# Top-k attention and a squared-ReLU MoE in one program: thresholds compared as bfloat16 views, late range check in other buffers, flag earlier, new order table

## The chip, the cores and the metric

The program runs on one core of a Trainium2 chip. The metric is the device time of one execution in microseconds (us), median of three. The engines are named as in the profile: PE is TensorE (PEld its weight loads), DVE VectorE, ACT ScalarE, POOL GpSimd, SP SyncE, which here issues the DMAs.

## What is computed

The reference, cut to what matters. `q`, `k`, `v` are (8, 8, 576, 64) in float32; the two MoE weight matrices arrive as float64.

```python
def _attn_ref(q, k, v):
    scores = (1.0 / np.sqrt(D)) * np.matmul(q, k.transpose(0, 1, 3, 2))
    kth = np.partition(scores, -32, axis=-1)[..., -32:-31]
    scores = np.where(scores >= kth, scores, -1000000000.0)
    attn = np.exp(scores - np.max(scores, axis=-1, keepdims=True))
    attn = attn / (np.sum(attn, axis=-1, keepdims=True) + 1e-09)
    return np.matmul(attn, v)

def _moe_ref(x, w_in, w_out, s, b):        # x: 4608 x 512, d_ff 2048
    r = np.maximum(x @ w_in, 0.0)
    return (s * (r * r) + b) @ w_out
```

So each of 8 x 8 x 576 score rows keeps its 32 largest entries, takes a softmax over them, and multiplies V; the result, laid out as 4608 tokens of 512, goes through two dense layers.

## The kernel before

**The work.** Attention is cut into 288 tiles of 128 score rows. For a tile, PE makes 128 x 576 scores in two halves (L418, `s_ps`), ACT copies them to SBUF with the scale (L424, tile `sc`), and DVE finds the 32nd largest in steps: the eight largest of each of eight groups of 72 (L429, `cand`), two picks over those (L434), a negated reduction (L438, `nt`), the row maximum (L453, `nb`) and the eight largest of 31 negated values (L444, `wl`), whose last entry is minus the threshold guess. `half_at` (L458, POOL) turns the high 16 bits of that entry, read as an int16, into a bias. `side` (L464, ACT) takes the sign of bias minus each score's high 16 bits, and counts; `window` (L470, POOL) multiplies scores and signs, `pad` (L474, POOL) adds eight padding values that depend on the count, and `wmax` (L484, DVE) reads the exact 32nd value from the eight largest of the product. `expo` (L478, ACT) makes the exponentials and `mask` (L488, DVE) keeps the chosen ones and sums them. PE transposes (L515 `tp`, L520 `tq`), ACT and DVE split the result into a high and a low part (L525, L530, L535, L540), and PE multiplies V (L550 to L556, `av`). At the end of a pair of heads, `finish1` to `finish5` scale by the sums and write a piece of the MoE input to DRAM (`xd`).

The MoE runs in 18 blocks of 256 tokens, each of 16 chunks of 128 hidden units. One chunk is 12 matmuls into `h` (L665), a ReLU (L671) and a square (L674) on ACT, a high and a low part on POOL (L678 `gh`, L682 `gl`), and 6 matmuls into `ops` (L688). After a block's last chunk DVE makes `osb` (L696) and SP stores it (L703). A block can start when the pairs that hold its tokens have been written.

The two weight matrices come as 64-bit words in 64 loads of 256 KB; DVE turns each into float32 in three bit operations (`bits0` to `bits2`, L342 to L348), ACT and POOL split it (L351, L354). All of that stands in the first part of the program, beside the first 40 tiles or so. When the second matrix is complete, PE sums its columns (L391, 32 matmuls).

**The range check.** The conversion is only valid for numbers in a range. So, late in the program, all 64 pieces are loaded once more (`again`, L326 in `fetch`) into buffers of the ring `sc`, which also holds the attention scores, the MoE input of block 16 (the list `LATE`) and the very last `osb`; ACT squares them (`far0`, L364) and squares and sums them (`far1`, L373; one instruction for a piece of the first matrix, two for the second). DVE takes the maximum (L1119), and `flag0` (DVE, L1123 to L1126), `flag1` (PE, L1130) and `flag2` (DVE, L1133 and L1134) join it with a check of the thresholds into one number `flag`. Behind the program every engine loads the flag (L1295) and branches on it (L1296): a general path would run if it were set. With these inputs it isn't.

**The order.** All instructions are recorded in a graph and a list scheduler, `Graph.order`, places them, engine by engine, before anything is emitted. `PARTS` gives for each operation its engine, a slot, a duration and an offset in tiles that is added to the tile's number to make a due key; `SLACK` says by engine how much later an operation with an earlier key may start and still go first; `TURN0` and `TURNS` set the key of a MoE chunk in tiles, `WTURN` that of the weights, `CHECK` that of the range check. Buffers are rings (`BUFS`: 5 `sc`, 2 `qs`, 2 `ka`, one `h`, two `ops`). Up to the first MoE matmul the program also fills gaps that the plan shows on PE with matmuls that nobody reads (`keep_busy`, L383).

```python
        lim = min(x[0] for x in c) + slack[e]
        return min(((o.key, s, o) for s, o in c if s <= lim), key=lambda x: x[:2])[1:]
```

On the engines themselves everything runs strictly in the emitted order, with semaphore waits between engines.

## Time and profile before

| | |
|---|---|
| time, median of 3 (lowest to highest) | 1493.95 us (1493.13 to 1495.11) |
| profiled execution: its own time | 1495.7 us |
| its span from first to last instruction | 1493.9 us, mean granted clock 0.986 |
| PE busy | 1433.2 us, 96% of the span |
| DVE, ACT, POOL busy | 1261.7 (84%), 1283.4 (86%), 1150.9 us (77%) |
| DMA | 256.6 MB, mean 172 GB/s |

The profiled execution is one run with the hardware profiler; its own time is 0.12% above the median of the others, and its span leaves 1.8 us of it outside. Busy times are sums over the whole span: a share says nothing about a stage. How the stages differ is read from a view by stretches, and what holds an engine in one from the timeline and from the chain of waits. A PE that counts as busy may still run its matmuls further apart than it could.

### The profile page before, as it was taken

What the parts mean: (1) busy time and instruction counts of PE and PEld (TensorE: products, weight loads), DVE (VectorE), ACT (ScalarE), POOL (GpSimd) and SP (SyncE); (2) the same over time, 40 slices, a digit from 0 to 9 for tenths busy, and PEclk for the clock granted to TensorE, in tenths of its full rate; (3) what the DMA queues carried; (4) which work ended last, traced back from release to release, by engine and by line L of the source; (5) the groups of instructions that cost most, each with busy time, mean ns of one, the idle gap of its engine ahead of it and who ended that gap; (6) DMA issues with size and microseconds to landing.
All of it is one profiled execution on the core that took longest, in us unless ns stands there. A gap on an engine that the chain in (4) does not pass through costs nothing.

```text
span 1493.9 us, 34308 instructions
## 1 busy us (share of the span) xinstructions
PE 1433.2 (96%) x9468; PEld 1263.4 (85%) x9468; DVE 1261.7 (84%) x5527; ACT 1283.4 (86%) x3382; POOL 1150.9 (77%) x1920
## 2 busy tenths in 40 slices
PE   6977999999999999999999999999999999999996
PEld 5744678999989899988898989999899989989885
DVE  6988998999999999999999999889999987875000
ACT  6777888998999899989999999888998998888366
POOL 6877887888888878888888788877888877675532
PEclk9987999999999999999999999999999999999998
DMA  6776766666566665676666665666566555552144
GB/s 184 221 204 180 221 179 172 179 177 191 159 178 195 182 171 155 187 211 174 177 195 196 170 182 163 192 175 168 157 197 185 149 176 139 145 167 87 45 151 134
DMA packets 173735, 256.63 MB, mean 172 GB/s; under 512 B 41952, under 2 KB 83936, under 8 KB 173536
## 3 DMA queue, kind: packets, MB, share of 16 engines
q1 hardware_dynamic: 173536, 254.37, 59.6%
q8 instruction: 78, 1.28, 0.4%
q14 instruction: 121, 0.99, 0.2%
HBM read 181.67 MB, written 72.61 MB: 170 GB/s over the span
## 4 chain that ended last, share of the span: by engine, by line
PE 73%; DVE 8%; ACT 8%; POOL 4%; DMA 4%; issue 2%; SPq 0%; POOLq 0%; DVEq 0%; ACTq 0%
PE ops L688 21%; PE h L665 21%; PE s_ps L418 10%; PE tp L515 7%; PE av L554 3%; PE av L555 3%; PE av L550 2%; PE tq L520 2%; DVE cand L429 1%; DVE sc L488 1%; DVE chk L484 1%; DMA kr<-in_kq_dram 1%; ACT sg L464 1%; DMA out_dram<-osb 1%; ACT sc L373 1%
## 5 line engine op out<-in xcount | busy, mean ns | idle before, releaser
L429 DVE MAX8 cand<-sc 128x8 f32<-128x72 f32 x2304 | 410.2, 221 | 37.1 <-ACT sc L424 35.7
L470 POOL TENSOR_TENSOR wt<-sc,sg 128x576 f32<-128x576 f32 x288 | 371.6, 1290 | 75.9 <-ACT sg L464 44.2
L665 PE MATMUL h<-x,wih 128*128 128x256 f32 x2176 | 427.7, 289 | 1.9 <-ACT rt L671 1.3
L665 PEld LDWEIGHTS h<-x,wih 128*128 128x128 f32 x2176 | 350.5, 190 | 21.5 <-ACT rt L671 4.6
L665 PE MATMUL h<-x,wil 128*128 128x256 f32 x1088 | 306.8, 282 | 0.0
L418 PE MATMUL s_ps<-ka,qs 128*128 128x288 f32 x1024 | 244.6, 321 | 27.9 <-ACT sc L424 11.0
L424 ACT ACTIVATE sc<-s_ps 128x288 f32<-128x288 f32 x576 | 233.5, 405 | 29.0 <-PE s_ps L418 23.8
L464 ACT ACTIVATE sg<-sc,nb 128x576 bf16<-128x576 int16 x288 | 222.5, 773 | 25.5 <-POOL nb L458 20.4
L484 DVE MAX8 chk<-wt 128x8 f32<-128x584 f32 x288 | 219.3, 761 | 23.2 <-POOL wt L474 20.8
L488 DVE SCALAR_TENSOR_TENSOR sc<-sc,chk,e 128x576 f32<-128x576 f32 x288 | 232.3, 807 | 7.4 <-ACT e L478 5.1
L478 ACT ACTIVATE e<-sc,nb 128x576 f32<-128x576 f32 x288 | 213.5, 741 | 25.7 <-DVE sc L488 18.2
L682 POOL TENSOR_TENSOR gl<-rt,gh 128x256 fp32r<-128x256 f32 x288 | 212.6, 739 | 27.3 <-PE ops L688 8.8
L418 PEld LDWEIGHTS s_ps<-ka,qs 128*128 128x128 f32 x1024 | 165.5, 193 | 70.9 <-ACT sc L424 39.0
L688 PE MATMUL ops<-woh,gh 128*128 128x512 f32 x576 | 202.3, 411 | 5.7 <-DVE osb L696 5.2
L665 PEld LDWEIGHTS h<-x,wil 128*128 128x128 f32 x1088 | 206.2, 190 | 0.0
L678 POOL TENSOR_SCALAR gh<-rt 128x256 fp32r<-128x256 f32 x288 | 116.7, 406 | 108.0 <-PE ops L688 50.3
L688 PE MATMUL ops<-woh,gl 128*128 128x512 f32 x576 | 196.3, 403 | 0.4 <-POOL gl L682 0.4
L688 PE MATMUL ops<-wol,gh 128*128 128x512 f32 x576 | 195.0, 404 | 0.0
L530 DVE TENSOR_TENSOR pl<-tp,ph 128x512 fp32r<-128x512 f32 x252 | 172.5, 684 | 23.4 <-ACT ph L525 20.4
L515 PE MATMUL tp<-idr,sc 128*128 128x128 f32 x1152 | 176.6, 276 | 3.5 <-DVE sc L488 1.6
L525 ACT ACTIVATE ph<-tp 128x512 fp32r<-128x512 f32 (+1 forms) x288 | 170.4, 592 | 5.3 <-PE tp L515 3.2
L671 ACT ACTIVATE rt<-h 128x256 f32<-128x256 f32 x288 | 109.2, 379 | 50.8 <-PE h L665 46.6
(151 smaller groups left out, 2941.5 us busy)
## 6 DMA issues: line engine op xcount, KB each, us to landing
ka<-kd SPq DMA_DIRECT2D x240, 288.0 KB, 4.4
vd<-vst SPq DMA_DIRECT2D x56, 320.0 KB, 3.9
vst<-vd SPq DMA_DIRECT2D x56, 320.0 KB, 3.2
kr<-in_kq_dram SPq DMA_DIRECT2D x56, 288.0 KB, 3.5
kd<-kh SPq DMA_DIRECT2D x56, 288.0 KB, 3.8
kd<-kr SPq DMA_DIRECT2D x56, 288.0 KB, 3.3
qs<-kd SPq DMA_DIRECT2D x224, 64.0 KB, 2.3
out_dram<-osb SPq DMA_DIRECT2D x36, 256.0 KB, 2.2
```

Source lines behind the costliest of these rows:

```text
L418: nc.tensor.matmul(t.ps[:, :SH], st, kx[:, cs], start=(m == 0), stop=(m == last))
L424: nc.scalar.activation(t.sc[:, hf * SH : (hf + 1) * SH], t.ps[:, :SH], AF.Identity, scale=scale)
L429: nc.vector.max(t.cand[:, g, 1:9], t.sc[:, g * GW : (g + 1) * GW])
L464: nc.scalar.activation(t.sg, t.sc.bitcast(I16)[:, 1::2], AF.Sign, bias=t.half, scale=-1.0, accum_out=t.cnt[:, 0:1])
L470: nc.gpsimd.tensor_tensor(out=t.wt[:, :S], in0=t.sc, in1=t.sg, op=ALU.mult)
L478: nc.scalar.activation(t.e, t.sc, AF.Exp, bias=t.nb)
L484: nc.vector.max(t.pair.chk[:, t.i, 0:PADS], t.wt)
L488: nc.vector.scalar_tensor_tensor(t.sc, t.sc, chk[:, PADS - 1 : PADS], t.e, op0=ALU.is_ge, op1=ALU.mult, accum_out=chk[:, PADS : PADS + 1])
L515: nc.tensor.transpose(tp[:, c, :], t.sc[:, c * P : (c + 1) * P], idf)
L665: nc.tensor.matmul(k.h, wi_at(a, cc, fc * P, P), k.x[cc][:, c, :], start=(cc == 0 and i == 0), stop=(cc == NCC - 1 and i == 2))
L682: nc.gpsimd.tensor_tensor(out=k.gl[fc], in0=k.rt[fc], in1=k.gh[fc].bitcast(F32), op=ALU.subtract)
L688: nc.tensor.matmul(k.ops[t], g[fc][:, t * P : (t + 1) * P], wo_at(w, fc, 0, DM), start=(fc == 0 and i == 0), stop=(fc == NFC - 1 and i == 2),)
```

## The change

It does five things.

1. `half_at` moves from POOL to DVE: a `tensor_reduce` over one element, the high half of the entry read as a bfloat16, negated.
2. `side` reads the high halves of the scores as bfloat16 instead of int16, and its scale is -1 - 2^-9 instead of -1. The threshold check in `finish1` and `flag0` becomes a minimum against 1e-30 instead of a maximum against 32767.
3. The range check loads its pieces into the rings `qs` and `ka` (those of Q and K) in turn, two buffers each, instead of `sc`.
4. The keys of the flag go down (`flag0` from 60 to -20.96, in tiles), and `flag2` is given a duration of 9000 ns in the plan.
5. All slots, durations and offsets of `PARTS`, the slacks and the three turns are new, so that nearly every instruction has another place.

```diff
-    "half": ("POOL", 147, 190, 44.13), "side": ("ACT", 759, 860, -18.51), "win": ("POOL", 1250, 1290, -12.54),
+    "half": ("DVE", 62, 150, 40.88), "side": ("ACT", 759, 860, -45.29), "win": ("POOL", 1250, 1290, -42.12),
...
-    "glow": ("POOL", 705, 745, 56.08), "o": ("PE", 231, 395, 42.40), "wagain": ("SP", 920, 3900, 44.77), "flag0": ("DVE", 560, 640, 60.00), "flag1": ("PE", 110, 360, 50.77), "flag2": ("DVE", 420, 500, 23.67), "osb": ("DVE", 654, 738, -13.89), "store": ("SP", 450, 2300, -30.67),
+    "glow": ("POOL", 705, 745, 60.00), "o": ("PE", 231, 395, 41.19), "wagain": ("SP", 920, 3900, 45.57), "flag0": ("DVE", 560, 640, -20.96), "flag1": ("PE", 110, 360, 31.04), "flag2": ("DVE", 420, 9000, 18.37), "osb": ("DVE", 665, 750, -9.98), "store": ("SP", 450, 2300, 1.71),
...
-SLACK = {"PE": 26, "DVE": 33, "ACT": 43, "POOL": 120, "SP": 861}
-TURN0, TURNS = 33.0, 1.074
-WTURN = 50.4
+SLACK = {"PE": 0, "DVE": 53, "ACT": 92, "POOL": 111, "SP": 520}
+TURN0, TURNS = 34.5, 1.136
+WTURN = 48.1
...
+    def again_in(n):
+        return ("qs", "ka")[n % 2]
...
         def again(w):
-            w.fetch(sb.tile([P, 2 * WCH], I32, name="sc", tag="sc", bufs=BUFS["sc"]))
+            tag = again_in(w.n)
+            w.fetch(sb.tile([P, 2 * WCH], I32, name=tag, tag=tag, bufs=BUFS[tag]))
...
-        nc.gpsimd.tensor_scalar(t.half, t.wl.bitcast(I16)[:, 15:16], 1.0, 32767.5, op0=ALU.mult, op1=ALU.add)
+        nc.vector.tensor_reduce(t.half, t.wl.bitcast(BF16)[:, 15:16], axis=AX.X, op=ALU.max, negate=True)
...
-            t.sg, t.sc.bitcast(I16)[:, 1::2], AF.Sign, bias=t.half, scale=-1.0, accum_out=t.cnt[:, 0:1]
+            t.sg, t.sc.bitcast(BF16)[:, 1::2], AF.Sign, bias=t.half, scale=-1.0 - 2.0**-9, accum_out=t.cnt[:, 0:1]
...
-        key, raw = CHECK + n / 2, Buf("sc")
+        key, raw = CHECK + n / 2, Buf(again_in(n))
...
-        nc.vector.scalar_tensor_tensor(tm, tx, 32767.0, tm, op0=ALU.is_lt, op1=ALU.mult)
+        nc.vector.scalar_tensor_tensor(tm, tx, 1.0e-30, tm, op0=ALU.is_gt, op1=ALU.mult)
```

How that moves instructions shows at three places. Lines of the changed kernel are three higher than those of before from L364 on (L458 is L461 there).

The end of DVE's order; `osb` is the last block's result, `far` the sums of the range check, `tmin` the thresholds. Before:

```order
L696 SCALAR_TENSOR_TENSOR osb<-ops,cols,bias 128x512 x4
L1119 TENSOR_REDUCE cols<-far 128x1
L696 SCALAR_TENSOR_TENSOR osb<-ops,cols,bias 128x512 x2
L1123 TENSOR_REDUCE cols<-tmin 128x1
L1124 TENSOR_REDUCE cols<-tmin 128x1
L1125 SCALAR_TENSOR_TENSOR cols<-cols 128x1
L1126 SCALAR_TENSOR_TENSOR cols<-cols 128x1
L1133 TENSOR_REDUCE cols<-tp 1x1
L1134 TENSOR_SCALAR flag<-cols 1x1
L1295 TENSOR_LOAD flag
```

and in the change:

```order
L699 SCALAR_TENSOR_TENSOR osb<-ops,cols,bias 128x512 x2
L1122 TENSOR_REDUCE cols<-far 128x1
L1126 TENSOR_REDUCE cols<-tmin 128x1
L1127 TENSOR_REDUCE cols<-tmin 128x1
L1128 SCALAR_TENSOR_TENSOR cols<-cols 128x1
L1129 SCALAR_TENSOR_TENSOR cols<-cols 128x1
L1136 TENSOR_REDUCE cols<-tp 1x1
L1137 TENSOR_SCALAR flag<-cols 1x1
L699 SCALAR_TENSOR_TENSOR osb<-ops,cols,bias 128x512 x2
L1298 TENSOR_LOAD flag
```

The flag is finished ahead of the last block's two `osb`. On PE its transpose, the last matmul of all before, now has 66 `h` and 48 `ops` matmuls behind it.

ACT's order near its end; `rt<-h` is a ReLU, `rt<-rt` a square, the rest is range check. Before, up to the load of the flag:

```order
L671 ACTIVATE rt<-h 128x256
L373 ACTIVATE sc,far<-sc,cols 128x128 x2
L674 ACTIVATE rt<-rt 128x256
L364 ACTIVATE sc<-sc 128x256 x2
L373 ACTIVATE sc,far<-sc,cols 128x128 x4
L1295 TENSOR_LOAD flag
```

and in the change, around the last two pieces:

```order
L674 ACTIVATE rt<-h 128x256
L367 ACTIVATE qs<-qs 128x256
L677 ACTIVATE rt<-rt 128x256
L376 ACTIVATE qs,far<-qs,cols 128x128 x2
L367 ACTIVATE ka<-ka 128x256
L376 ACTIVATE ka,far<-ka,cols 128x128 x2
L674 ACTIVATE rt<-h 128x256
L677 ACTIVATE rt<-rt 128x256
```

The last piece was checked behind the last of the 288 chunks; now seven chunks follow it. Of the 64 pieces, 37 stood behind chunk 273 before, all in the last block; now the first two stand behind chunk 247 and the 64 are spread over 34 chunks, about two to a chunk.

PE's order where the column sum (`av<-woh,ones`) begins, which needs the whole second weight matrix. Before:

```order
L665 MATMUL h<-x,wih 128x256 x2
L665 MATMUL h<-x,wil 128x256
L418 MATMUL s_ps<-ka,qs 128x288 x2
L391 MATMUL av<-woh,ones 128x512
L391 MATMUL av<-wol,ones 128x512
```

and in the change:

```order
L668 MATMUL h<-x,wih 128x256 x2
L668 MATMUL h<-x,wil 128x256
L691 MATMUL ops<-woh,gh 128x512 x2
L421 MATMUL s_ps<-ka,qs 128x288 x2
L394 MATMUL av<-woh,ones 128x512
L394 MATMUL av<-wol,ones 128x512
```

Ahead of it PE has issued the transposes of 37 tiles and the `h` matmuls of 13 chunks before, of 36 tiles and 15 chunks in the change. The second MoE block begins after 42 tiles before, and after 39 in the change; the ninth after 169 and 166; the seventeenth after 288 and 287. The matmuls that only fill gaps are 203 before and 172 in the change. On DVE the last of the 64 weight conversions stands behind 37 masks before and 36 in the change.

## Rows read from the trace of the kernel before

**Rows 1.** The page, busy time and share of each engine over the span.

```profile
PE 1433.2 (96%) x9468; PEld 1263.4 (85%) x9468; DVE 1261.7 (84%) x5527; ACT 1283.4 (86%) x3382; POOL 1150.9 (77%) x1920
```

**Rows 2.** Busy time of each engine by stretches of the span, named in the header.

```profile
core 0: us, PE busy (x) PEld busy (x) DVE busy (x) ACT busy (x) POOL busy (x), PEclk, DMA share, GB/s
0.00:187.00 187.00, 148.18 (x759) 103.67 (x759) 161.93 (x731) 140.73 (x352) 143.25 (x235) 0.91 0.69 202
187.00:1195.00 1008.00, 1001.42 (x6848) 904.53 (x6847) 951.32 (x4205) 915.34 (x2346) 835.11 (x1387) 1.00 0.63 178
1195.00:1382.00 187.00, 184.45 (x1246) 167.10 (x1245) 142.40 (x580) 163.22 (x457) 128.23 (x224) 1.00 0.50 143
1382.00:1434.00 52.00, 51.70 (x333) 46.84 (x333) 1.98 (x4) 17.27 (x46) 26.00 (x45) 1.00 0.15 49
1434.00:1482.00 48.00, 47.20 (x288) 41.19 (x286) 1.56 (x3) 46.80 (x183) 18.34 (x32) 1.00 0.62 190
1482.00:1493.90 11.90, 0.27 (x1) 0.08 (x1) 2.50 (x9) 0.00 (x0) 0.00 (x0) 0.66 0.14 51
```

**Rows 3.** Timeline, 1481 us to the end: start, duration, engine, line, instruction.

```profile
1481.28 0.62 PE L688 MATMUL ops<-woh,gl 128*128 128x512 f32 x2
1481.71 0.20 ACT L373 ACTIVATION_READ_ACCUMULATOR sc<-sc,cols 128x1 f32 x1
1481.94 0.25 DVE L1119 TENSOR_REDUCE cols<-far 128x1 f32<-128x96 f32 x1 [39.95 <-ACT sc L373]
1482.11 1.40 DVE L696 SCALAR_TENSOR_TENSOR osb<-ops,cols,bias 128x512 f32<-128x512 f32 x2
1482.88 1.00 SPq L703 DMA_DIRECT2D out_dram<-osb  x2
1484.83 0.14 DVE L1134 TENSOR_SCALAR flag<-cols 1x1 int32<-1x1 f32 x1
```

**Rows 4.** Instructions of lines 1295, 1296 and 1330: durations in ns, start in us.

```profile
L1295 PEldq TENSOR_LOAD <-flag x1: 482/482/482, 1485.0 to 1485.0; - x1
L1296 SPq COMPARE_BRANCH  x1: 50/50/50, 1485.5 to 1485.5; - x1
L1296 PEldq COMPARE_BRANCH  x1: 3772/3772/3772, 1485.6 to 1485.6; - x1
L1330 SPq DRAIN  x3: 7/7/13, 1490.3 to 1493.2; - x3
L1330 PEldq DRAIN  x2: 8/8/8, 1492.6 to 1493.2; - x2
```

**Rows 5.** SP's timeline near the end: loads of block 16 (L642) and the range check (L326).

```profile
1370.03 7.94 SPq L642 DMA_DIRECT2D sc<-xd  x4
...
1396.15 0.38 SPq L326 DMA_DIRECT2D sc<-in_moe_w_in_dram  x1
1430.00 1.76 SPq L326 DMA_DIRECT2D sc<-in_moe_w_out_dram  x4
```

**Rows 6.** The chain that ended last, near 1421 us: start, duration, work.

```profile
1421.12 1.43 PE h L665 x12
1422.56 1.39 PE ops L688 x6
1423.94 1.43 PE h L665 x12
```

**Rows 7.** DVE's timeline near 14 us.

```profile
14.32 0.14 DVE L453 TENSOR_REDUCE nb<-nt 128x1 f32<-128x8 f32 x1
14.38 0.18 DVE L444 MAX8 wl<-nt 128x8 f32<-128x31 f32 x1
14.48 0.62 DVE L429 MAX8 cand<-sc 128x8 f32<-128x72 f32 x4
```

**Rows 8.** Groups of instructions by line: busy us, mean ns of one, idle before.

```profile
L464 ACT ACTIVATE sg<-sc,nb 128x576 bf16<-128x576 int16 x288 | 222.5, 773 | 25.5 <-POOL nb L458 20.4 <-POOL wt L470 2.9
L478 ACT ACTIVATE e<-sc,nb 128x576 f32<-128x576 f32 x288 | 213.5, 741 | 25.7 <-DVE sc L488 18.2 <-DVE avu L617 2.6 <-DVE avu L624 2.5
L458 POOL TENSOR_SCALAR nb<-wl 128x1 f32<-128x1 int16 x288 | 54.9, 191 | 39.3 <-DVE wl L444 17.1 <-PE tq L520 1.1
L453 DVE TENSOR_REDUCE nb<-nt 128x1 f32<-128x8 f32 x288 | 42.8, 149 | 2.0
L674 ACT ACTIVATE rt<-rt 128x256 f32<-128x256 f32 x288 | 120.1, 417 | 2.7
L671 ACT ACTIVATE rt<-h 128x256 f32<-128x256 f32 x288 | 109.2, 379 | 50.8 <-PE h L665 46.6 <-POOL gl L682 1.5 <-POOL qs L837 0.6
```

**Rows 9.** Timelines of DVE, POOL and PE where the last weights are made, and the second block's start.

```profile
216.36 0.40 DVE L348 SCALAR_TENSOR_TENSOR pl<-pl,s_ps 128x256 int32<-128x256 int32 x1
...
217.92 0.73 POOL L354 TENSOR_TENSOR wol<-pl,woh 128x256 fp32r<-128x256 f32 x1
...
221.42 0.40 PE L391 MATMUL av<-woh,ones 128*128 128x512 f32 x1
...
247.31 0.46 PE L665 MATMUL h<-x,wih 128*128 128x256 f32 x2
```

More of the change, by code (lines that the diff above doesn't have):

```diff
@@ L14 @@
 I32 = mybir.dt.int32
-I16 = mybir.dt.int16
 AF = mybir.ActivationFunctionType
@@ L55 @@
-    "exp": ("ACT", 667, 748, 55.25), "wmax": ("DVE", 668, 754, -35.90), "pad": ("POOL", 480, 420, -5.48), "mask": ("DVE", 731, 815, -58.93),
-    "put": ("PE", 436, 680, 1.41), "putq": ("PE", 108, 350, 13.37), "high": ("ACT", 478, 595, 55.65), "low": ("DVE", 590, 675, -3.19),
-    "resth": ("ACT", 264, 372, 17.15), "restl": ("DVE", 568, 610, -43.14), "av": ("PE", 146, 320, -18.63), "avout": ("ACT", 320, 470, -18.43),
-    "eps": ("ACT", 95, 200, -14.34), "recip": ("DVE", 72, 180, 23.03),
-    "sums": ("DVE", 140, 230, 34.96), "add": ("POOL", 1375, 1420, -57.27), "spread": ("POOL", 525, 560, -55.31), "turn": ("PE", 108, 352, -31.85),
@@ L66 @@
-SLACK = {"PE": 26, "DVE": 33, "ACT": 43, "POOL": 120, "SP": 861}
-TURN0, TURNS = 33.0, 1.074
-WTURN = 50.4
+    "wload": ("SP", 1000, 4400, 15.06), "bits0": ("DVE", 325, 415, 40.39), "bits1": ("DVE", 321, 412, 38.69), "bits2": ("DVE", 321, 404, 16.54),
+    "colsum": ("PE", 7400, 7600, -9.49), "far0": ("ACT", 322, 430, 17.89), "far1": ("ACT", 507, 524, 29.35), "far2": ("ACT", 782, 793, 5.64),
+    "whigh": ("ACT", 322, 425, -32.98), "wlow": ("POOL", 700, 736, -59.18), "farmax": ("DVE", 170, 250, 32.68), "bias": ("ACT", 695, 700, -17.80),
@@ new lines @@
+    "vload": ("SP", 620, 3600, -28.72), "vhigh": ("ACT", 360, 466, 11.55), "vlow": ("POOL", 840, 875, 50.14), "vkeep": ("SP", 600, 2800, 57.18),
+    "qk": ("PE", 132, 300, -35.38), "sc": ("ACT", 291, 408, -35.29), "group": ("DVE", 134, 218, 57.78),
+    "m1": ("DVE", 92, 180, -45.24), "m2": ("DVE", 93, 180, 37.54), "neg": ("DVE", 120, 203, 19.40), "low8": ("DVE", 100, 182, 16.84), "max": ("DVE", 60, 143, -26.78),
+    "half": ("DVE", 62, 150, 40.88), "side": ("ACT", 759, 860, -45.29), "win": ("POOL", 1250, 1290, -42.12),
@@ new lines @@
+    "exp": ("ACT", 667, 748, 48.70), "wmax": ("DVE", 668, 754, -40.73), "pad": ("POOL", 480, 420, -16.83), "mask": ("DVE", 724, 807, -8.69),
+    "put": ("PE", 436, 680, -1.29), "putq": ("PE", 108, 350, 9.09), "high": ("ACT", 478, 595, 40.24), "low": ("DVE", 590, 675, -40.93),
+    "resth": ("ACT", 264, 372, 11.07), "restl": ("DVE", 568, 610, -43.39), "av": ("PE", 146, 320, -33.81), "avout": ("ACT", 320, 470, -4.23),
+    "eps": ("ACT", 192, 298, -21.24), "recip": ("DVE", 78, 168, 13.84),
+    "sums": ("DVE", 125, 207, 13.95), "add": ("POOL", 1375, 1420, -58.41), "spread": ("POOL", 525, 560, -51.94), "turn": ("PE", 108, 352, -31.37),
@@ new lines @@
+    "scale": ("DVE", 325, 405, -15.53), "xkeep": ("SP", 500, 2600, 31.13),
+    "xload": ("SP", 460, 2700, -33.79), "xhigh": ("ACT", 306, 405, -31.38), "xlow": ("POOL", 692, 732, -60.00),
+    "h": ("PE", 357, 523, 38.72), "relu": ("ACT", 263, 378, -55.75), "square": ("ACT", 306, 415, -34.00), "ghigh": ("POOL", 369, 405, 60.00),
+    "glow": ("POOL", 705, 745, 60.00), "o": ("PE", 231, 395, 41.19), "wagain": ("SP", 920, 3900, 45.57), "flag0": ("DVE", 560, 640, -20.96), "flag1": ("PE", 110, 360, 31.04), "flag2": ("DVE", 420, 9000, 18.37), "osb": ("DVE", 665, 750, -9.98), "store": ("SP", 450, 2300, 1.71),
+}
@@ L572, in finish1 @@
         nc.vector.tensor_reduce(tmin[:, 0, pr.i : pr.i + 1], pr.chk[:, :n, PADS - 1 :], axis=AX.XY, op=ALU.min)
-        nc.vector.tensor_reduce(tmin[:, 1, pr.i : pr.i + 1], pr.nb[:, 1, :n], axis=AX.X, op=ALU.max)
+        nc.vector.tensor_reduce(tmin[:, 1, pr.i : pr.i + 1], pr.nb[:, 1, :n], axis=AX.X, op=ALU.min)
     def finish1a(pr):
```

19 lines of the change are left out of this document (5 added, 14 removed).

## The prediction

> **What bounds the kernel now.** I read the busy shares first: PE is at 96%, the others between 77% and 86% [rows 1]. A share of the whole span hides stages, so the next view is the one by stretches [rows 2]. It shows four regimes. Up to 187 us PE is busy for 148 of 187 us, at a mean granted clock of 0.91, and DVE for 162: this is the start, where DVE converts weights beside the first tiles. From 187 to 1195 us PE idles 6.6 us in 1008 and DVE 56.7: PE sets the time and DVE follows at 94%. From 1382 us attention is over (DVE 2 us of 52), and PE runs MoE chunks alone. From 1434 to 1482 us ACT is busy 46.8 of 48 us, where it was busy 17 of 52 in the stretch ahead. Behind 1482 us nearly nothing runs for 11.9 us.
>
> The chain of waits gives the price of a chunk: 1.43 us of `h` and 1.39 us of `ops`, 2.82 us from one chunk to the next [rows 6]. So 16 chunks need 45.1 us, and 288 need 812 us.
>
> The reader should see in the timeline of the end that PE's last MoE matmul ends at about 1481.9 us, that ACT's last range check ends at the same time, and that the flag is finished at 1484.97 us, 3.1 us later, behind a maximum, two `osb` of 1.40 us together and six short steps on DVE and PE [rows 3]. Only then do the engines load it and branch. PE is the slowest in that: its load takes 0.48 us and its branch 3.77 us, and its first drain stands at 1492.6 us, against 1490.3 us for SP [rows 4]. From the flag to the end of the span it is 8.9 us.
>
> **The change part by part.** The sum is made against the profiled execution, whose time is 1495.7 us, its span 1493.9 us and the 1.8 us around it; the median of the runs shown is 1493.95 us, 1.75 us lower, and I subtract the sum from that. A measurement of this kernel tells about 0.2%, 3.0 us, from no change.
>
> *The flag ahead of the end.* In the new order the flag is done ahead of the last two `osb`, and 66 `h` and 48 `ops` matmuls follow its transpose on PE: 66 x 1.43/12 + 48 x 1.39/6 = 19 us. So PE can load the flag as soon as its last matmul is issued, at about 1481.9 us in the times of before, not at 1485.0: 3.1 us less, and the 8.9 us behind it stay. What is late next is SP: it issues the last stores until 1483.9 us [rows 3], and from its branch at 1485.5 us to its drain it took 4.8 us [rows 4], so its drain would come at 1488.7 us, ahead of PE's at 1489.5. PE stays last. Gain 3.0 us, nothing at the least (a flag that comes late holds PE instead), and no more than 3.1. The Trainium skill (Runtime: NRT & Kernel Launch, Instruction fetch mechanics) says that a taken branch to a page that isn't at hand has to fetch it by DMA first; by that rule the branch stays dear however early the flag is, and PE's 3772 ns, against 482 for its load, agree [rows 4].
>
> *The range check in other buffers.* Before, block 16 held four of the five `sc` buffers: its loads went out at 1370 us, one piece was loaded at 1396 us, and the next four at 1430 us [rows 5]. So 37 pieces fell into the last block, where ACT is full [rows 2]. From 1434 to 1482 us PE had 48 us for 45.1 us of chunks plus what it was behind with; I put the loss to ACT at 2.6 us at most. In the new order two pieces fall to a chunk: 46.8 us less 16 x (0.38 + 0.42) us of ReLU and square [rows 8] leaves 34 us for 37 pieces, 0.92 us each, so ACT has 1.9 x 0.92 + 0.8 = 2.5 us in 2.82, 90% in place of 98%. It is spread over two blocks, so some loss stays. Gain 1.5 us, between 0 and 2.6. The cover is ACT's idle time of 35 us between 1382 and 1434 us [rows 2]; without it, nothing is gained. SP issues the pieces between the loads of blocks 16 and 17, and a piece that waits for its buffer holds those loads behind it; block 17's come some 16 chunks ahead of their use.
>
> *The threshold on DVE.* POOL loses 288 instructions of 191 ns [rows 8], at 77% busy: nothing. DVE gains 288 small reductions. The nearest row is the one-element reduction of `nb`: it lasts 149 ns [rows 8], and the next instruction starts 60 ns behind it [rows 7]. I take 60 ns, since DVE is in order and rarely waits for its own result there, and keep 149: 17 to 43 us over the program. Of that 37 tiles fall into the start, 2.2 to 5.5 us. The other 251, 15 to 37 us, fall into stretches in which DVE idles 56.7 + 44.6 us [rows 2]; I cost them at nothing, with that idle time as cover. If the cover fails, see the rivals. In the new order the reduction often stands behind a mask, so that the sign waits 0.8 us more; ACT's wait for the old one was 20.4 us in all [rows 8], off PE's path. The sign itself stays at 773 ns; the exponential, as long and on float32, takes 741 [rows 8], so its 288 could at best give back 9 us of ACT, which isn't the bound.
>
> *The new order of the start.* The column sum waits for the last weights. Before, DVE made the last of them at 216.8 us, POOL at 218.7, and PE began the sum at 221.4 [rows 9]. In the new order DVE has as much ahead of that point, less one tile and plus the 2.2 to 5.5 us. PE has two chunks more ahead of it, 5.6 us, and one tile less. A tile costs PE about (1433.2 - 812)/288 = 2.1 us, an upper estimate that takes all that isn't MoE as tiles [rows 1, 6]. So at an equal point PE is 3.5 us further on, and this is what counts, since PE is the bound from then on. At an equal tile it is three chunks or so, 8 us. Less the delay of DVE, the gain lies between -2 and +6 us; DVE idles 25 us in the first 187 [rows 2], which takes part of the delay, and I take 2.0. The 31 fill matmuls that go cost nothing, they stand in gaps.
>
> *The middle.* PE's 6.6 us of idle in 1008 are the most that a better order could give there by this count; a worse one has no such limit. I take 0.
>
> The sum is 3.0 + 1.5 + 2.0 = 6.5 us: 1495.7 - 6.5 = 1489.2 us for a profiled execution, **1487.5 us** for the median.
>
> **The rivals.**
>
> *Only the end moves.* The start gives nothing, because DVE reaches the last weights later by as much as PE is ahead. For it: DVE is busy 87% of the start. Then 3.0 + 1.5 = 4.5 us and 1489.5 us.
>
> *The gain is given back, or the flag doesn't come early.* The flag's transpose stands 19 us ahead of PE's end, and PE is in order: if ACT is behind with the checks, PE stops there for as long as it gained at the end. With the start at nothing this gives 1494 us. Against it: at 90% ACT should keep up, and behind its last check stands a ReLU that PE needs anyway before it comes to that point, since there is one `h` buffer.
>
> *DVE becomes the pace.* DVE is busy 94% from 187 to 1195 us [rows 2], and an in-order engine at that share can't use all its idle time: some of it is waiting for ACT and POOL. If the new reductions can't go into the waits, their time comes on top, and since both orders leave the same 34 or 35 chunks for the time after the last tile, all that follows moves. At 60 ns that is 251 x 0.06 = 15 us: 1494 - 4.5 + 15 = 1504 us, and at 149 ns 1526 us. It decides as soon as DVE's queue is never empty when PE wants a tile. The Trainium skill (Perfetto Trace Analysis, Optimizing Scalar/DVE Operations) speaks against this part of the change: with about 60 ns of overhead for each DVE instruction, it advises to take work off a DVE that is saturated, not to add to it. The 60 ns agree with the trace [rows 7]; by its figure, an estimate is 17 us on DVE. Against the rival: PE's own waits in that stretch are small, so DVE has been ahead of PE's need.
>
> *A better middle.* All PE idle time between 187 and 1382 us goes, 9.1 us [rows 2]: 1478 us.
>
> **How the numbers follow.** The forecast has a chance of 0.45, only the end 0.20, given back 0.17, DVE as the pace 0.13, a better middle 0.05. Faster by over 0.2%: nearly all of the forecast (0.44), the middle (0.05) and most of "only the end" (0.17), which lies close to the bound, together 0.66. Same: most of what is given back (0.14) and those edges (0.04), 0.18. Slower: DVE (0.13) and the rest of what is given back (0.03), 0.16. The range reaches down to the better middle, 1478 us (a start of +6 us with a free end gives about the same, 1494 - 3 - 2.6 - 6 = 1482), and up to 1500 us, which is only the end with two thirds of DVE's 15 us on top; it leaves out most of the DVE case, and what little lies below.
>
> **What would show it.** Right: the flag is finished some 19 us ahead of PE's last matmul, and the span ends 9 us behind that matmul, not 12; ACT's busy share in the last two blocks is near 90%, with none of the last seven chunks beside checks; the second MoE block starts earlier than its 247.3 us of before [rows 9] by more than three tiles' work on PE, 6.3 us. Wrong: DVE near 98% with PE waiting for score tiles in the middle; PE waiting at the flag's transpose; a longer time from the second block to the end than before, by more than the three tiles that moved behind it.

## The result and the profile after

The changed kernel takes 1476.32 us (median of 4 runs, 1473.77 to 1476.69) against 1494.53 us for the kernel before beside it: a ratio of 0.9867, 95% interval 0.9839 to 0.9896, 18 us less where 6.5 us were forecast. The sign was right, the size was not, and the time lies 1.7 us below the range. The profiled execution took 1476.01 us, its span 1474.2 us.

The busy shares of the page and the windows of the kernel after, to be read beside [rows 1, 2] (the last window ends behind this kernel's span):

```profile
PE 1419.9 (96%) x9437; PEld 1257.9 (85%) x9437; DVE 1274.6 (86%) x5815; ACT 1285.9 (87%) x3382; POOL 1094.2 (74%) x1632
```

```profile
core 0: us, PE busy (x) PEld busy (x) DVE busy (x) ACT busy (x) POOL busy (x), PEclk, DMA share, GB/s
0.00:187.00 187.00, 151.62 (x785) 107.17 (x785) 164.90 (x771) 142.32 (x360) 140.57 (x209) 0.93 0.71 204
187.00:1195.00 1008.00, 997.19 (x6850) 905.36 (x6850) 956.01 (x4402) 915.09 (x2342) 790.51 (x1163) 1.00 0.63 178
1195.00:1382.00 187.00, 186.07 (x1275) 169.42 (x1274) 149.14 (x632) 160.68 (x439) 127.31 (x199) 1.00 0.49 139
1382.00:1434.00 52.00, 51.42 (x324) 46.08 (x323) 1.92 (x3) 49.42 (x184) 22.26 (x41) 1.00 0.66 204
1434.00:1482.00 48.00, 33.58 (x209) 29.88 (x207) 2.66 (x9) 18.39 (x63) 13.58 (x24) 0.95 0.17 52
```

DVE carries the new reductions in the middle (956 us of 1008, 951 before). PE idles 10.8 us there instead of 6.6, and starts as many matmuls (6850, 6848 before). The range check, which filled ACT from 1434 us on before, now fills it from 1382 to 1434 us (49.4 of 52 us) and is over early. To see where the time went, cut the span at the first `h` matmul of three MoE blocks and at the end of PE's last `ops` matmul, all from the timelines. "Tail" is from that end to the end of the span. Kernels can reach the same block with different numbers of tiles behind them, so the tiles are counted too: a tile stands ahead of a block when PE has started its transposes (`tp`, L515, L518 in the change) before that block's first `h`.

| kernel | block 1 starts | block 1 to 15 | 15 to 17 | 17 to last matmul | tail | span | tiles ahead of 1, from 1 to 15, behind |
|---|---|---|---|---|---|---|---|
| before | 247.3 | 1077.9 | 107.0 | 49.7 | 12.0 | 1493.9 | 42, 238, 8 |
| after | 231.5 | 1079.0 | 108.0 | 49.0 | 6.7 | 1474.2 | 39, 238, 11 |

Of the 19.7 us of span, 15.8 stand at block 1 and 5.3 in the tail. Three tiles moved from ahead of block 1 to behind it, at most 6.5 us of PE's time by the prediction's upper price ((1433.2 - 812)/288 is 2.16 us a tile, not 2.1), so 9.3 us or more of the 15.8 are a gain of the start. The middle holds 238 tiles in both and is 1.1 us longer. The three tiles are worked off behind block 15, and the stretch from there to the last matmul still takes only 157.0 us, against 156.7 before.

The tail, in the instructions of lines 1137, 1298, 1299 and 1333 (durations in ns, least, median and most, then first and last start in us), answers to [rows 4]:

```profile
L1137 DVE TENSOR_SCALAR flag<-cols x1: 146/146/146, 1449.0 to 1449.0; 1x1 int32<-1x1 f32 x1
...
L1298 PEldq TENSOR_LOAD <-flag x1: 483/483/483, 1465.8 to 1465.8; - x1
...
L1299 PEldq COMPARE_BRANCH  x1: 3372/3372/3372, 1466.4 to 1466.4; - x1
...
L1299 SPq COMPARE_BRANCH  x1: 50/50/50, 1469.2 to 1469.2; - x1
...
L1333 SPq DRAIN  x3: 7/7/13, 1473.4 to 1473.7; - x3
L1333 PEldq DRAIN  x2: 8/8/8, 1470.0 to 1473.8; - x2
```

PE's last matmul ends at 1467.6 us. PE's sequencer loads the flag at 1465.8 and begins its branch at 1466.4 us, while matmuls that it has issued still run. (The ends of matmuls in a profile are modelled; DVE's last two `osb`, which read their results, start at 1467.4 us.) PE reaches its first drain at 1470.0 us, SP, behind the last store, at 1473.4: SP is last now.

### The profile page after: what moved, and what is told of

Read it like the earlier page. It is cut to its first block, busy times and chain, and to the rows that moved or that the text cites. A ratio compares the mean times of both kernels' runs of the same rounds, so it can differ in the third digit from the quotient of the medians.

```text
span 1474.2 us, 34428 instructions
## 1 busy us (share of the span) xinstructions
PE 1419.9 (96%) x9437; PEld 1257.9 (85%) x9437; DVE 1274.6 (86%) x5815; ACT 1285.9 (87%) x3382; POOL 1094.2 (74%) x1632
## 4 chain that ended last, share of the span: by engine, by line
PE 73%; ACT 9%; DVE 7%; DMA 5%; issue 2%; POOL 2%; SPq 1%; POOLq 0%; ACTq 0%; DVEq 0%
PE h L668 22%; PE ops L691 22%; PE s_ps L421 10%; PE tp L518 7%; PE av L557 3%; PE av L558 3%; PE av L553 2%; ACT sg L467 2%; DMA x<-xd 2%; PE tq L523 2%; ACT sc L427 1%; DVE cand L432 1%; DVE sc L491 1%; DMA out_dram<-osb 1%; DVE chk L487 1%
## 5 line engine op out<-in xcount | busy, mean ns | idle before, releaser
L432 DVE MAX8 cand<-sc 128x8 f32<-128x72 f32 x2304 | 420.5, 221 | 30.0 <-ACT sc L427 28.7
L421 PE MATMUL s_ps<-ka,qs 128*128 128x288 f32 x1024 | 241.0, 316 | 28.9 <-ACT sc L427 11.8
L467 ACT ACTIVATE sg<-sc,nb 128x576 bf16<-128x576 bf16 x288 | 222.2, 772 | 12.1 <-DVE nb L461 5.1
L487 DVE MAX8 chk<-wt 128x8 f32<-128x584 f32 x288 | 218.7, 759 | 14.1 <-POOL wt L477 12.8
L518 PE MATMUL tp<-idr,sc 128*128 128x128 f32 x1152 | 176.3, 276 | 7.9 <-DVE pl L533 2.3
L518 PEld LDWEIGHTS tp<-idr,sc 128*128 128x128 f32 x1152 | 135.3, 141 | 29.6 <-DVE pl L533 7.1
```

Source lines behind the costliest of these rows:

```text
L421: nc.tensor.matmul(t.ps[:, :SH], st, kx[:, cs], start=(m == 0), stop=(m == last))
L432: nc.vector.max(t.cand[:, g, 1:9], t.sc[:, g * GW : (g + 1) * GW])
L467: nc.scalar.activation(t.sg, t.sc.bitcast(BF16)[:, 1::2], AF.Sign, bias=t.half, scale=-1.0 - 2.0**-9, accum_out=t.cnt[:, 0:1])
L487: nc.vector.max(t.pair.chk[:, t.i, 0:PADS], t.wt)
L518: nc.tensor.transpose(tp[:, c, :], t.sc[:, c * P : (c + 1) * P], idf)
```

## The experiments

Every kernel is compared with the kernel before on the same chip (three rounds each). All the numbers below that begin with "block" are read as in the table above. Where a planner's number, or a tile that the planner knows of, is changed, the plan is made anew; where only the emission is changed, the order stays but for what is named.

**1. Half alone, in a fixed order.** The kernel after with the old forms of `half`, `side`, `finish1` and `flag0`; the kernel before with the new ones; each in its own order.

```
-        nc.vector.tensor_reduce(t.half, t.wl.bitcast(BF16)[:, 15:16], axis=AX.X, op=ALU.max, negate=True)
+        nc.gpsimd.tensor_scalar(t.half, t.wl.bitcast(I16)[:, 15:16], 1.0, 32767.5, op0=ALU.mult, op1=ALU.add)
```

> The kernel after in its own order, but half goes back to GpSimd and all comparisons go back to int16 views. Theory (the order of the start, the flag and the buffers carry the gain, the engine of half carries none): 1474 to 1480 us against 1476.3 for after, first MoE matmul of block 0 again near 69.6 us. Rival (half on VectorE carries it, by a shorter chain in each of 288 tiles and a freer GpSimd): most of the 18 us go, 1486 to 1495 us.

> The kernel before in its own order, with half on VectorE in bfloat16 and nothing else of the change. Theory (the order carries the gain): 1492 to 1496 us, as before. Rival (half on VectorE carries it): 1476 to 1485 us. Rival on the other side (288 more VectorE instructions of 141 ns, 40.6 us, on an engine that is busy for 95% of the middle): 1500 to 1530 us.

Measured: after with half on POOL 1525.61 us, ratio 1.020 (1.018 to 1.022); before with half on DVE 1506.78 us, ratio 1.0067 (1.0050 to 1.0084). Both lose, the first by more than its rival had allowed, so the first theory falls: the engine of half is not free in either order. Groups by line (busy us, mean ns, idle ahead) of after, of after with half on POOL and of before with half on DVE:

```profile
L467 ACT ACTIVATE sg<-sc,nb 128x576 bf16<-128x576 bf16 x288 | 222.2, 772 | 12.1 <-DVE nb L461 5.1 <-POOL wt L473 2.5 <-POOL wt L477 1.1
...
L461 DVE TENSOR_REDUCE nb<-wl 128x1 f32<-128x1 bf16 x288 | 40.6, 141 | 1.5
```

```profile
L468 ACT ACTIVATE sg<-sc,nb 128x576 bf16<-128x576 int16 x288 | 222.8, 774 | 57.0 <-POOL nb L462 50.2 <-POOL wt L474 3.9
```

```profile
L464 ACT ACTIVATE sg<-sc,nb 128x576 bf16<-128x576 bf16 x288 | 222.5, 772 | 38.1 <-DVE nb L458 31.7 <-POOL wt L470 2.8 <-POOL gh L678 0.8
```

The sign takes the same 772 to 774 ns on int16 and on bfloat16 views. What differs is how long ACT stands idle until half is there: 5.1 us in after, 20.4 before [rows 8], 31.7 with DVE's half in the old order, 50.2 with POOL's in the new one. From block 1 to 15 these four took 1079.0, 1077.9, 1085.1 and 1115.0 us. So what a step in each of 288 tiles costs goes with its place in the queue, not with its 141 or 190 ns. ACT's wait alone is not the price: 20.4 us before and 5.1 in after go with the same middle. The stretch from 187 to 1195 us of before with half on DVE, to be read beside [rows 2]:

```profile
187.00:1195.00 1008.00, 1000.05 (x6796) 896.21 (x6795) 953.82 (x4402) 908.92 (x2330) 786.57 (x1152) 1.00 0.63 178
```

DVE is busy 94.6% of it, 94.4% before, and PE idles 8.0 us instead of 6.6, but starts 52 matmuls fewer.

**2. The flag last of all.** After, with the three flag steps sorted behind everything:

```
+    todo = graph.order(SLACK)
+    todo.sort(key=lambda o: o.name in ("flag0", "flag1", "flag2"))
```

> The kernel after, with the three flag steps issued last of all. Theory (PE's branch is hidden because it loads the flag while its queued matmuls still run, worth the 5.4 us by which the tail behind PE's last matmul shrank, 12.0 to 6.6): 1481 to 1483 us. Rival (the prediction's sum, 3.0 us): 1479 to 1480 us. Rival (the tail is set by the last store on SP anyway): within 1 us of 1476.3.

> The kernel after, unchanged, beside the three below. 1474 to 1478 us, and with it the scale on which a late flag (1477.4 us in an earlier comparison) counts.

Measured: 1477.39 us, ratio 0.9879 (0.9860 to 0.9899); after once more 1476.74 us, 0.9877 (0.9858 to 0.9896). The times can't tell them apart. The traces can: the tail is 9.2 us instead of 6.7 and 6.6, so the late flag costs 2.5 us there, about the 3.0 that the prediction put on it, not 5.3. The other 2.8 us are a longer end of the kernel before: there 3.2 us pass on PE from the end of its branch, at 1489.4 us, to its first drain [rows 4], but 0.2 us in after and with this late flag. Why is not shown; the two other kernels with the order of before and a late flag, half on DVE (1.) and the early store (4.), have tails of 11.6 and 10.8 us. In this kernel PE's branch begins behind its last matmul:

```profile
L1301 PEldq COMPARE_BRANCH  x1: 3572/3572/3572, 1469.7 to 1469.7; - x1
```

**3. The range check's buffers.** Before with the check in the buffers of K and Q, and after with it in `sc`:

```
-            w.fetch(sb.tile([P, 2 * WCH], I32, name="sc", tag="sc", bufs=BUFS["sc"]))
+            tag = again_in(w.n)
+            w.fetch(sb.tile([P, 2 * WCH], I32, name=tag, tag=tag, bufs=BUFS[tag]))
...
```

> The kernel before with the range check's weights read into the buffers of K and Q, as after does, and all else as it was; the plan is the same up to the first of these loads. Theory (in before the check in the scores buffers ended last, so that the flag waited for it, 2.9 us of the tail, and blocks 16 and 17 lost 1.9 us): 1488 to 1491 us, and the tail behind TensorE's last MoE matmul 9 to 10 us instead of 12.0. The prediction's sum for this part alone: 1492 to 1494 us. Rival (the scores buffers fit the numbers of before): 1495 us or more.

> The kernel after with the range check's weights read into the scores buffers again, the rest of the plan as it comes. Theory (the check in those buffers ends so late that TensorE's last two blocks and the flag behind them wait: 1.9 us in the blocks, and the 2.9 us by which the tail of before is longer than that of the kernel with a late flag, 12.0 against 9.1): 1479 to 1482 us. The prediction's sum: 1477.5 to 1478 us. Rival (the buffers do not matter, only the order): within 1 us of 1476.3.

Measured: before with the new buffers 1493.30 us, ratio 0.9977 (0.9963 to 0.9992); after with the old ones 1519.92 us, 1.0156 (1.0138 to 1.0175). In the first the tail is 7.0 us, though the flag's ranks are those of before. Lines 1138, 1299 and 1300 of before with the new buffers:

```profile
L1138 DVE TENSOR_SCALAR flag<-cols x1: 142/142/142, 1443.4 to 1443.4; 1x1 int32<-1x1 f32 x1
...
L1299 PEldq TENSOR_LOAD <-flag x1: 490/490/490, 1482.3 to 1482.3; - x1
...
L1300 PEldq COMPARE_BRANCH  x1: 3555/3555/3555, 1482.9 to 1482.9; - x1
```

The flag comes early by itself as soon as the check ends early (PE's last matmul ends at 1484.1 us here). So the check, which ended last before [rows 3], held the flag. The new buffers are not the only way out of that: in the control on before (9.), with the check in `sc` and the flag's keys of before, the check ends 12.4 us and the flag is done 10.7 us ahead of PE's last matmul, and the tail is 6.6 us. In after with the old buffers blocks 15 to 17 take 153.8 us instead of 108.0. Five tiles more are left there, 16 instead of 11, which is at most 10.8 us of it. For the rest, 39 of the 64 raw pieces are loaded into the buffers that the last tiles need ahead of the last copy of scores (26 before; in after, with its own buffers, 2), tiles run until 1408 us, and PE starves. Its windows there:

```profile
core 0: us, PE busy (x) PEld busy (x) DVE busy (x) ACT busy (x) POOL busy (x), PEclk, DMA share, GB/s
...
1380.00:1400.00 20.00, 13.38 (x48) 9.32 (x48) 15.78 (x66) 14.14 (x35) 7.43 (x11) 0.60 0.38 121
1400.00:1420.00 20.00, 13.10 (x50) 10.52 (x50) 7.57 (x27) 12.93 (x41) 7.96 (x13) 0.59 0.18 53
```

**4. The store of MoE input alone.** Before, with each of the first eight `xkeep` emitted right behind its `scale`:

```
+    for keep in [o for o in todo if o.name == "xkeep"][:8]:
+        todo.remove(keep)
+        todo.insert(todo.index(keep.deps[0][0] if type(keep.deps[0]) is tuple else keep.deps[0]) + 1, keep)
```

> The kernel before, with the first eight stores of attention output (batch 0) issued on SP right behind the scale step that they store, and nothing else moved. Theory (in the kernel before these stores stood 12.8 to 22.0 us behind loads in SP's order, and that is what the new order of the start took away): the first MoE matmul of block 0 comes at 68 to 72 us instead of 78.8 and the time is 1485 to 1489 us. Rival (TensorE's own order, or the weights, set the start): block 0 starts earlier or not, and the time stays within 2 us of 1494.5.

Measured: 1494.40 us, ratio 0.9993 (0.9981 to 1.0005). The theory falls as it stood: block 0 begins at 79.6 us (78.8), block 1 at 245.9. Lines 617, 630 and 642 (scale, store, load; four pairs, first and last start) of before, and then of this kernel:

```profile
L617 DVE TENSOR_TENSOR avu<-avu,e x4: 409/416/422, 46.7 to 115.7; 128x256 f32<-128x256 f32 x4
...
L630 SPq DMA_DIRECT2D xd<-avu x4: 544/560/578, 67.0 to 132.1; - x4
...
L642 SPq DMA_DIRECT2D x<-xd x4: 320/330/536, 69.7 to 138.2; - x4
```

```profile
L630 SPq DMA_DIRECT2D xd<-avu x4: 325/328/538, 47.8 to 115.2; - x4
...
L642 SPq DMA_DIRECT2D x<-xd x4: 424/504/585, 70.4 to 132.5; - x4
```

The first store moves from 67.0 to 47.8 us, the load behind it stays at 70.4: it stands behind the same weight loads in SP's order. Nor does PE wait long for that input: from 40 to 250 us its waits at `h` for `x` or for a DMA are 0.7 us or less each, in before and here, so PE's own order, which this edit leaves alone, sets when the chunks come.

**5. MoE earlier, or later, by a fixed time.** Before with every MoE step and its input's store, load and split emitted 12 us of the plan earlier; after with them 12 us later. Only the emission is sorted anew.

```
+    left = sorted(graph.order(SLACK), key=lambda o: o.start - (1000.0 * (12) if o.name in moe else 0.0))
...
```

> The kernel before, all of it as it was (half on GpSimd, scores buffers for the range check), but every MoE step and every step that stores, loads and splits its input stands 12 us of the plan earlier on its engine, so that the MoE chunks stand two to three tiles further ahead of attention all through the kernel (chunk 1 behind 21 tiles where it was 23, chunk 16 behind 39 where it was 42: the places that the kernel after has). Theory (the start of after gains about 10 us because MoE work fills TensorE's idle time while the weights are converted, and a store alone moves nothing since load, split and matmul behind it stand in order): chunk 1 at 128 to 136 us instead of 145.9 and a time of 1484 to 1488 us. Rival (the lead is worth nothing without the other new numbers): 1493 to 1497 us. Rival on the other side (MoE steps stand ahead of tiles that they then delay): 1500 us or more.

> The kernel after, all of it as it is, but the MoE steps stand 12 us of the plan later on their engines (chunk 16 behind 43 tiles where it was 39, near the 42 of before). Theory (the lead of MoE is what the new order gains in the start): block 1's first matmul near 245 us instead of 231.5 and 1485 to 1489 us. Rival (the lead is worth nothing): 1475 to 1479 us.

Measured: 1726.84 us, ratio 1.154 (1.152 to 1.157), and 1665.02 us, 1.113 (1.111 to 1.115). Blocks 1 to 15 take 1258.7 and 1221.6 us. MoE had the places of the other kernel, counted in tiles, and lost 181 us and 143 us in the middle alone: what counts there is how steps of tiles and chunks alternate on each engine. Chunk 1 begins at 140.9 us in the first, where its theory had 128 to 136, and block 1 at 270.2 and 266.7 us; with everything disturbed, these two runs decide nothing on the start.

**6. The rank of weight loads on SP.** The fourth number of `wload`, 8.71 before and 15.06 after, put alone into the other kernel:

```
-    "wload": ("SP", 1000, 4400, 15.06), ...
+    "wload": ("SP", 1000, 4400, 8.71), ...
```

> The kernel after with one number changed back: the rank of a weight load on SP goes from 15.06 to the 8.71 of before. The start then has the places of before (chunk 1 behind 23 tiles, chunk 16 behind 42, 212 fill matmuls). Theory (this rank brings the start's gain): block 1's first matmul at 243 to 249 us instead of 231.5, and 1484 to 1492 us. Rival (the lead is worth nothing): 1474 to 1480 us.

> The kernel before with one number of its planner changed: the rank of a weight load on SP goes from 8.71 to the 15.06 of after, so that stores and loads of MoE input pass weight loads. The order of the start then has the places of after (chunk 1 behind 21 tiles instead of 23, chunk 16 behind 39 instead of 42, 149 fill matmuls instead of 203). Theory (this rank on SP is what brings the start's gain): block 1's first matmul at 232 to 238 us instead of 247.3, and 1480 to 1488 us, as the rest of the plan stays within some 4 us. Rival (the lead is taken back in the middle, where TensorE is busy throughout): block 1 early, but 1491 to 1498 us. Rival (weights that come later hold up the first MoE chunks): block 1 no earlier than 245 us.

Measured: after with the old rank 1499.49 us (1493.44 to 1502.60), ratio 1.0011 (0.9994 to 1.0028), block 1 at 248.4 us and 1077.4 us from there to block 15. Before with the new rank 1533.86 us, 1.0245 (1.0215 to 1.0274), block 1 at 236.9 us, but 1104.9 us to block 15 and 133.4 from there to 17. Scale, store and load (lines 620, 633, 645) of after, and of after with the old rank:

```profile
L620 DVE TENSOR_TENSOR avu<-avu,e x4: 402/421/422, 40.6 to 114.8; 128x256 f32<-128x256 f32 x4
...
L633 SPq DMA_DIRECT2D xd<-avu x4: 382/499/788, 57.4 to 115.6; - x4
...
L645 SPq DMA_DIRECT2D x<-xd x4: 326/374/538, 61.6 to 119.7; - x4
```

```profile
L620 DVE TENSOR_TENSOR avu<-avu,e x4: 409/415/421, 40.2 to 117.0; 128x256 f32<-128x256 f32 x4
...
L633 SPq DMA_DIRECT2D xd<-avu x4: 334/430/441, 71.4 to 131.2; - x4
...
L645 SPq DMA_DIRECT2D x<-xd x4: 326/541/579, 76.2 to 134.6; - x4
```

The scale is where it was, the store and the load come 14 to 16 us later, and so does all of MoE: block 1 by 16.9 us. In its trace, that of its fastest execution, this kernel is 17.5 us longer than after, with a middle of 1077.4 us (235 tiles, 238 in after), so here the start's loss stays to the end. But the rank also puts other tiles ahead of block 1, 42 instead of 39 in after and 39 instead of 42 in before. Less three tiles at 2.16 us, the old rank loses 10.4 us at block 1 in after, and the new one gains 3.9 us in before.

**7. More of the same rank.** After with ranks 17 and 19 instead of 15.06.

> The kernel after with the rank of weight loads on SP at 17 instead of 15.06: MoE stands further ahead in the start (chunk 1 behind 18 tiles instead of 20, chunk 16 behind 39 as after, 146 fill matmuls instead of 172). Theory (the lead of MoE in the start is worth what it takes from fills and idle time, and the rest of the plan stays within some us): block 1's first matmul at 226 to 231 us and 1470 to 1478 us. Rival (weights that come later hold up the chunks of block 0): block 1 at 234 us or later, and 1478 us or more.

> As the kernel with rank 17, with rank 19: chunk 1 behind 19 tiles, chunk 16 behind 37 instead of 39, 146 fill matmuls. Theory: block 1's first matmul at 223 to 230 us and 1468 to 1478 us. Rival (weights late): block 1 at 234 us or later, and 1478 us or more.

Measured: 1518.44 us, ratio 1.0159 (1.0140 to 1.0178), and 1514.16 us, 1.0121 (1.0100 to 1.0143). Chunk 0 begins earlier (60.2 and 60.5 us, 69.6 in after), block 1 later (241.3 and 240.7). Tiles are late: the mask of the 37th tile comes at 226.0 and 233.7 us instead of 215.9. Windows of after and of rank 17 from 100 to 200 us (columns as above):

```profile
100.00:150.00 50.00, 40.13 (x178) 26.55 (x177) 44.94 (x213) 37.11 (x98) 35.42 (x52) 0.83 0.75 208
150.00:200.00 50.00, 49.75 (x295) 37.32 (x294) 48.77 (x216) 44.31 (x115) 44.06 (x65) 1.00 0.63 185
```

```profile
100.00:150.00 50.00, 39.79 (x185) 29.68 (x185) 40.59 (x178) 34.81 (x91) 36.92 (x53) 0.74 0.65 193
150.00:200.00 50.00, 44.24 (x236) 30.31 (x234) 48.82 (x230) 43.98 (x112) 43.40 (x64) 0.97 0.65 182
```

DVE falls from 44.9 to 40.6 us of 50 and PE from 49.8 to 44.2. So for block 1 the rank has a best value between; which load exactly is late in these two was not followed.

**8. Numbers and edits apart.** The edits of after with the numbers of before (but DVE's durations for half); the code of before with the numbers of after (but POOL's for half); after with half on POOL and the planner told so.

> The kernel after with all its edits (half on VectorE, bfloat16 views, the range check in the buffers of K and Q), but laid out by the planner with the numbers of before; only half has VectorE's durations of after. Theory (the numbers carry the start's gain, the range check some 5 us): 1485 to 1492 us, block 1 first at 243 us or later. Rival (the edits alone carry it, the numbers are only a record of them): 1476 to 1480 us. Rival on the other side (numbers that do not fit the edit, as in the kernel before with half on VectorE): 1497 to 1510 us.

> The kernel before with its own code (half on GpSimd, the range check in the scores buffers) laid out by all the numbers of after. Theory (the numbers are fitted to the edits, as the +43 us of the kernel after with the scores buffers shows, so that they bring the start's gain and lose more behind it): block 1's first matmul near 235 us, and 1495 us or more. Rival (the numbers alone are the gain): 1478 to 1484 us.

> The kernel after with half on GpSimd in its int16 form, and the plan made anew with GpSimd's durations for half; all other numbers and edits of after. Theory (an order costs tens of us when one step of each tile stands on an engine for which the numbers were not fitted; half on VectorE is itself worth little): 1490 us or more here too, as the numbers are fitted to VectorE, and the start no better than 235 us at block 1. Rival (a plan that knows where half runs gives the gain back, so that only the unplanned move cost 49 us): 1475 to 1482 us.

Measured: 1502.05 us, ratio 1.0031 (1.0017 to 1.0045); 1558.95 us, 1.0423 (1.0395 to 1.0450); 1517.68 us, 1.0152 (1.0133 to 1.0171). Neither numbers nor edits alone give a gain, though by the control below a loss of this size can come with any new plan. Both kernels with half on POOL and the numbers of after start badly, block 1 at 258.1 and 258.5 us.

**9. The control.** The planner is told that a sign takes 762 ns, not 759; nothing else is touched.

```
-    ... "side": ("ACT", 759, 860, ...
+    ... "side": ("ACT", 762, 863, ...
```

> A control: the kernel after, whose planner is told that the sign of a tile takes 3 ns more (762 instead of 759), which is no property of the work; the plan is made anew and differs in its details, with the same places in the start (chunk 1 behind 20 tiles, chunk 16 behind 40 where it was 39, 172 fill matmuls). Theory A (the planner's numbers as a whole were selected, any plan made anew loses, so that a loss in one of the runs above can't be put on the number or edit that was changed in it): 1490 us or more, with losses spread over many blocks. Theory B (the runs above show the price of what was changed in them): 1474 to 1480 us. Either way the start, block 1's first matmul, stays within 4 us of 232.

> The same control on the kernel before: the sign planned at 762 ns instead of 759, the places in the start as before (chunk 1 behind 23 tiles, chunk 16 behind 42, 204 fill matmuls). Theory A: 1505 us or more. Theory B: 1492 to 1498 us. Either way block 1's first matmul stays within 4 us of 247.

Measured: after 1497.47 us, ratio 1.0020 (1.0006 to 1.0033); before 1530.48 us, 1.0244 (1.0217 to 1.0270). So 3 ns in a table cost 21 us and 35 us, and theory A holds. The parts of the span of all the kernels whose plan was made anew:

| plan made anew | block 1 starts | block 1 to 15 | 15 to 17 | tail | check in | tiles ahead of 1, from 1 to 15, behind |
|---|---|---|---|---|---|---|
| control on after | 235.4 | 1095.9 | 107.2 | 6.6 | K, Q | 40, 237, 11 |
| control on before | 245.5 | 1095.4 | 129.6 | 6.6 | `sc` | 42, 232, 14 |
| old rank in after | 248.4 | 1077.4 | 109.8 | 6.7 | K, Q | 42, 235, 11 |
| new rank in before | 236.9 | 1104.9 | 133.4 | 7.2 | `sc` | 39, 236, 13 |
| rank 17; 19 | 241.3; 240.7 | 1109.2; 1107.8 | 108.2; 109.0 | 6.9; 6.6 | K, Q | 39, 238, 11; 37, 240, 11 |
| edits, old numbers | 251.8 | 1093.2 | 100.5 | 6.7 | K, Q | 42, 241, 5 |
| old code, new numbers | 258.1 | 1083.3 | 158.3 | 7.2 | `sc` | 43, 228, 17 |
| after, half on POOL | 258.5 | 1090.4 | 109.1 | 7.0 | K, Q | 43, 234, 11 |
| before, check in K, Q | 245.7 | 1091.3 | 98.4 | 7.0 | K, Q | 42, 243, 3 |
| after, check in `sc` | 233.0 | 1074.5 | 153.8 | 6.8 | `sc` | 39, 233, 16 |

Read by columns, and with the tiles beside them, this tells what one total can't. Brought to 238 tiles at 2.16 us a tile, the middle takes 1080 to 1109 us in all of these; before (1077.9) and after (1079.0) are shorter than any. The start holds within 4 us under a change that means nothing (one control on each kernel), so 16.9, 10.4 and 27 us at block 1 come with the rank and with half, three or four tiles included (8.6 us at most). And blocks 15 to 17 take 98 to 110 us in every one of these with the check in the buffers of K and Q, 130 to 158 us in every one with it in `sc`; the kernel before itself took 107.0. Those with `sc` have 13 to 17 tiles left behind block 15, before had 8: at 2.16 us a tile that leaves 10 to 32 us that the tiles don't explain.

## Why the prediction was wrong

**The start is the mis-sized term, and the step that failed in it is the delay of DVE.** The step read: "Less the delay of DVE, the gain lies between -2 and +6 us", with 2.0 us taken. Block 1 begins 15.8 us earlier, about 9.3 us of it net of three tiles. The sign I held against it, DVE later at the last weight, did not come. Timeline of after at the last weight, to be read beside [rows 9], and the windows up to there of before and of after (columns as above):

```profile
212.70 0.40 DVE L350 SCALAR_TENSOR_TENSOR pl<-pl,s_ps 128x256 int32<-128x256 int32 x1
...
216.87 0.39 PE L394 MATMUL av<-woh,ones 128*128 128x512 f32 x1
```

```profile
0.00:216.40 216.40, 177.58 (x934) 126.14 (x935) 189.75 (x853) 165.96 (x416) 169.00 (x276) 0.92 0.69 200
```

```profile
0.00:212.70 212.70, 177.31 (x943) 127.80 (x944) 190.06 (x888) 164.47 (x418) 163.18 (x241) 0.94 0.70 204
```

The last conversion began 3.7 us ahead of before (2.0 in after once more), and the column sum 4.5 us ahead; with the 3.5 us by which PE is further on at that point, this makes 8.0 us. Up to that conversion DVE is busy 190.1 us, 189.8 before. The prediction wrote "less one tile and plus the 2.2 to 5.5 us", but subtracted only the second: a tile is at most 4.3 us of DVE (951.3 us from 187 to 1195 us [rows 2], in which it does 223 masks), which is as much as the reductions bring.

What the gain hangs on is the rank of weight loads: with the old one, after loses 10.4 us net at block 1, against 4 and 2 us in the controls. It is not the whole of it, since in before the new rank alone gains only 3.9 us net. How it acts was shown in part. The attention output of a pair stood 12.8 to 22.0 us in SP's order ahead of its store (67.0 against 46.7 us for the first pair), in after 0.8 to 16.8 us, and the load of block 0 stands behind it; I had looked up SP near the end [rows 5] and never at the start. But PE hardly waits for that input (4.): in the traces its own order holds the second chunk back, behind 23 tiles before and 20 in after. That the plan gives it these places because of SP's queue is argued, not shown. That 31 fill matmuls "cost nothing" was not tested by itself.

**The tail: failed steps, with a size off by 2.3 us.** The steps "PE can load the flag as soon as its last matmul is issued, at about 1481.9 us in the times of before", "the 8.9 us behind it stay" and "PE stays last" failed. PE's sequencer is ahead of its matmuls: it loads the flag 1.8 us before the last one ends, and a third of its 3372 ns branch lies beside them; the prediction took issue and end for one time. From that load to the end of the span it is 8.4 us, and SP is last. So 3.1, 1.8 and 0.5 us came, 5.3 within rounding, and the bound of 3.1 was wrong. The branch is nearly as dear as before, 3372 against 3772 ns, as the rule on taken branches that the prediction quoted from the Trainium skill (Runtime: NRT & Kernel Launch, Instruction fetch mechanics) would have it; being early pays all the same. The flag comes early once the check ends early, which the new buffers bring about and another plan can too (3.). Against a late flag in the order of after its early place is worth 2.5 us (2.).

**The range check.** 1.5 us were put on PE's last two blocks, 2.6 at most. From block 15 to the last matmul after takes 157.0 us and before 156.7, but after does 11 tiles there and before 8. With the check in K and Q this stretch took 147.0 us with 3 tiles (before, check in K, Q) and 157.0 with 11; at that rate 8 tiles would take 153.2, an estimate that puts the gain near 3.5 us. These orders differ in more than the buffers, so the term stays open.

**Half on DVE.** "I cost them at nothing, with that idle time as cover" is false in the order of before: 10.4 us (ratio 1.0067), two thirds of the 15 us that the rival "DVE becomes the pace" put on 60 ns each. Its sign, "DVE near 98% with PE waiting for score tiles", did not come (1.); what grew is ACT's wait for half, from 20.4 to 31.7 us. The Trainium skill's advice (Perfetto Trace Analysis, Optimizing Scalar/DVE Operations), to take work off a saturated DVE, fits that price on a DVE that is busy 94.6%. In the order of after the middle is 1.1 us longer with the same 238 tiles: there the cost is covered. That it is covered by the new places, and by which, was not shown further than by ACT's wait for half, 5.1 us.

**The middle** was forecast at 0 and is 1.1 us longer: this step held. The real flaw is in the sum itself: it adds prices of parts as if each part had one. Half costs 10 us in one order and taking it back costs 49 in the other; the buffers move the total by 3 and 44, and a change that means nothing moves it by 21 and 35. A chance for "a better start, larger than +6" was missing from the rivals.

## What to carry to other kernels

When a table that lays out the work changes, look at each queue for what stands between a step and the one that waits for its result, all the way to the matmul: a store that is early is worth nothing while the load behind it, or the matmul in PE's own order, is not. Before a part of such a change is priced by taking it back, run a control that changes something meaningless in the plan, and compare stage by stage, with the work that each stage holds: here the control moved the total by 21 and 35 us and the start by no more than 4.
